# A retention-normalised attention feeding four sparse attention experts: gate logits folded into the state, new load runs, two-bank PSUM tiles and interleaved score row groups

## The chip, the cores and the metric

The kernel runs on one core of one Trainium2 chip. The metric is device time in microseconds of one launch; of the kernel before, three runs gave a median of 517.08 us (516.87 to 517.32).

## What is computed

Two blocks follow each other, in float32. B = 8 batches, H = 8 heads, S = 576 tokens, head dimension 64, E = 4 experts of head dimension 64, D = 512.

```python
# attention without softmax, per batch b and head h
kv  = einsum('bhsd,bhse->bhde', k, v)             # a 64x64 state per head
out = einsum('bhsd,bhde->bhse', q, kv)
x   = out / sqrt(mean(out*out, -1) + 1e-6) * g_norm      # -> x: B, S, H*64

# experts: the two largest of four gate logits per token
logits = x @ w_gate ; w = softmax over the top 2 logits
for e in range(4):
    qe, ke, ve = x @ wq[e], x @ wk[e], x @ wv[e]
    a  = softmax(causal(qe @ ke.T / 8))
    y += w_e * (a @ ve @ wo[e])                   # w_e = 0 where e is not chosen
```

All four experts are computed for all tokens, and the gate (zero where an expert is not chosen) scales their outputs.

## The kernel before

Every batch goes through two generators. `attention` (L157) is the first block, `moe_block` (L260) the second, and `moe_final` (L451) the output projection of a batch, put off until the next one. `run_interleaved` (L467) issues `moe_block` of batch b and calls one step of `attention` of batch b+1 for every four of its steps; before that loop `attention` of batch 0 runs alone (L489), and in the last round `moe_block` has no partner. Every engine takes its instructions in the order that results; the framework, which sets all semaphores, moves single instructions a little where its own plan finds them not ready.

`load_qkv` (L145) brings one batch's q, k and v by five token blocks (four of 128, one of 64): fifteen DMAs on SP's queue, all in runs of one token of one head, 256 bytes. Batch b+2 is loaded when batch b begins. The weights are loaded and scaled by g_norm before the first batch (L112 to L143).

`attention`: for each of four head pairs it transposes q (p_qT, L170), copies it to SBUF on ACT (L174), accumulates k-transposed times v over the tokens (p_kv, L177, 64 of 128 rows in the last block) and copies the two diagonal 64x64 blocks to kv2_all on DVE (L186, L187). Then, for each token block: out (p_out, L212, eight instructions of 128 columns, as a float32 product is two), squares on ACT (L220), sums on DVE (L222), mean plus epsilon (L229), the power -0.5 on POOL (rstd, L238), and the product x_tok on DVE (L245). Two blocks later `flush_one` (L196) transposes x_tok (p_xT), ACT copies it (L202), and DVE rounds it to xT_r (L203), the form in which the experts' matmuls read it.

`moe_block`: the gate logits are a float32 product of wg_f and xT (p_lt, L266), four rows high, transposed back to tokens (p_log, L276); L285 to L309 make the gates. Then follow ve of all experts (p_v, L322), `moe_final` of the batch before (p_y, L455; y_sb on DVE, L463; the store, L464), and for each of two expert pairs: projections (p_proj, L346, segments of 512 and 64 columns), copies to qTp and kTp (L358), scores transposed (p_sc, L371: first all of one expert, on rows 0 to 63, then all of the other, on rows 64 to 127, nine each), exponentials on ACT (L378), the causal mask on POOL (L384), then per query block and expert p_O (L409), a reciprocal (L417) and the scaling by reciprocal and gate (O_sc, L418), and a transpose (p_OT, L430) which ACT copies to OT_all (L446). Pair 1 starts its projections when pair 0 is through.

PSUM is one pool of eight one-bank buffers (L90).

## Time and profile before

| | us |
|---|---|
| median of three runs | 517.08 |
| span of the profiled execution | 515.2 |
| TensorE busy (matmul) | 400.2 |
| weight loads, beside them | 285.5 |
| DVE busy | 197.3 |
| ACT busy | 173.9 |
| POOL busy | 124.2 |

The profile is of one execution; no separate time of it is given beside its span of 515.2 us, and the median of the runs lies 1.9 us above that. Engines run side by side, so their times do not add up. PE is the matmul side of TensorE, PEld its weight loads. "Idle before <- X" is time in which the engine had nothing to do until X was finished. The input's 28.3 MB and the output's 9.4 MB pass over SP's queue.

### The profile page before, as it was taken

How to read it: one execution, taken by the hardware profiler on the slowest of the kernel's cores; microseconds unless marked ns; L12 is line 12 of the kernel's file. 1: busy time of each engine (PE TensorE's matmuls, PEld its weight loads, DVE VectorE, ACT ScalarE, POOL GpSimd, SP SyncE). 2: the span in 40 equal slices, each digit the busy share in tenths (PEclk: the TensorE clock that was granted, in tenths of full speed). 3: DMA queues.
4: the chain of work that ended last, by engine and by line, in shares of the span. 5: the costliest groups of instructions: out<-in, count | busy, mean ns of one | idle time of the engine just before them, and what ended most of it. 6: DMA issues, size and time to landing. Idle time of an engine off the chain costs nothing.

```text
span 515.2 us, 7111 instructions
## 1 busy us (share of the span) xinstructions
PE 400.2 (78%) x2472; PEld 285.5 (55%) x2472; DVE 197.3 (38%) x717; ACT 173.9 (34%) x569; POOL 124.2 (24%) x234
## 2 busy tenths in 40 slices
PE   0066696959969899679968799679968799679884
PEld 0055285726758467554757368454757367564661
DVE  1104334354252342543443442543433542543523
ACT  0013143611514215252246215251245215251440
POOL 3004202430132302351043302351043302340220
PEclk9999799869955599797988699796988699796866
DMA  8999908801390015900295014900200011000202
GB/s 168 206 195 204 206 13 160 118 1 42 108 205 15 2 41 128 199 2 0 92 182 96 1 41 119 207 3 0 87 7 1 1 42 52 0 2 1 93 0 92
DMA packets 125107, 40.31 MB, mean 78 GB/s; under 512 B 120208, under 2 KB 120208, under 8 KB 125072
## 3 DMA queue, kind: packets, MB, share of 16 engines
q1 hardware_dynamic: 125072, 39.87, 38.8%
q8 instruction: 19, 0.31, 0.3%
q14 instruction: 16, 0.13, 0.1%
HBM read 30.42 MB, written 9.44 MB: 77 GB/s over the span
## 4 chain that ended last, share of the span: by engine, by line
PE 56%; DVE 13%; POOL 11%; ACT 8%; issue 5%; DMA 3%; SPq 3%; POOLq 0%; DVEq 0%; ACTq 0%
POOL rstd L238 11%; PE p_kv L177 10%; PE p_lt L266 9%; PE p_proj L346 9%; PE p_out L212 5%; PE p_v L322 4%; PE p_qT L97 4%; DVE O_sc L418 4%; PE p_O L409 4%; PE p_y L455 3%; DVE x_tok L245 3%; PE p_sc L371 3%; ACT PT L378 3%; DVE sumsq L222 3%; ACT sq L220 2%
## 5 line engine op out<-in xcount | busy, mean ns | idle before, releaser
L384 POOL TENSOR_SCALAR_AFFINE_SELECT PT<-PT 128x128 bf16<-128x128 bf16 (+1 forms) x160 | 44.0, 290 | 195.4 <-ACT PT L378 191.0
L238 POOL TENSOR_TENSOR rstd<-msq,neg_half 128x8 f32<-128x8 f32 (+1 forms) x40 | 65.8, 1645 | 102.3 <-DVE msq L229 98.8
L378 ACT ACTIVATE PT<-p_sc 128x64 bf16<-128x64 f32 (+5 forms) x288 | 65.1, 341 | 14.5 <-PE p_sc L371 13.8
L409 PE MATMUL p_O<-vext,PT 128*128 128x65 bf16 (+2 forms) x480 | 43.5, 232 | 22.0 <-DVE x_tok L245 20.3
L371 PE MATMUL p_sc<-qTp,kTp 64*128 64x64 f32 (+5 forms) x288 | 49.3, 305 | 6.7 <-ACT kTp L358 4.2
L212 PE MATMUL p_out<-kv_all,qT_all 128*128 128x128 f32 (+1 forms) x320 | 52.8, 318 | 2.1 <-ACT PT L378 2.1
L245 DVE TENSOR_TENSOR x_tok<-p_out,rstd 128x512 f32<-128x512 f32 (+1 forms) x40 | 27.6, 689 | 65.3 <-POOL rstd L238 65.3
L177 PE MATMUL p_kv<-v_b,k_b 128*128 128x128 f32 (+1 forms) x320 | 51.7, 300 | 0.0
L97 PE MATMUL p_OT<-ident_b,O_sc 128*128 128x128 bf16 (+1 forms) x80 | 21.8, 273 | 38.4 <-DVE O_sc L418 38.1
L97 PE MATMUL p_qT<-ident_f,q_b 128*128 128x128 f32 (+1 forms) x160 | 28.6, 288 | 29.1 <-DMA q_b<-in_q_dram 29.1
L266 PE MATMUL p_lt<-xT,wg_f 128*4 128x64 f32 (+1 forms) x128 | 50.9, 564 | 0.0
L418 DVE TENSOR_SCALAR O_sc<-p_O,invr,gate 128x64 bf16<-128x64 f32 (+1 forms) x160 | 49.8, 334 | 1.6 <-PE p_OT L97 0.6
L409 PEld LDWEIGHTS <-PT 128*128 128x128 bf16 (+2 forms) x480 | 31.8, 124 | 30.8 <-POOL PT L384 11.1
L371 PEld LDWEIGHTS p_sc<-qTp,kTp 64*128 64x128 f32 (+1 forms) x288 | 39.3, 188 | 16.0 <-ACT kTp L358 5.8
L212 PEld LDWEIGHTS p_out<-kv_all,qT_all 128*128 128x128 f32 (+1 forms) x320 | 44.8, 209 | 5.8 <-ACT PT L378 3.5
L220 ACT ACTIVATE sq<-p_out 128x512 f32<-128x512 f32 (+1 forms) x40 | 23.8, 596 | 66.4 <-PE p_out L212 58.9
L222 DVE TENSOR_REDUCE sumsq<-sq 128x8 f32<-128x512 f32 (+1 forms) x40 | 27.2, 680 | 47.8 <-ACT sq L220 47.8
L177 PEld LDWEIGHTS p_kv<-v_b,k_b 128*128 128x128 f32 (+1 forms) x320 | 41.5, 194 | 6.3 <-issue 0.2
L174 ACT COPY qT_all<-p_qT 128x512 f32<-128x512 f32 x64 | 23.0, 419 | 61.5 <-PE p_qT L97 61.5
L186 DVE COPY kv_all<-p_kv 64x64 f32<-64x64 f32 x32 | 6.9, 216 | 90.1 <-PE p_kv L177 87.3
L97 PEld LDWEIGHTS p_qT<-ident_f,q_b 128*128 128x128 f32 (+1 forms) x160 | 19.4, 143 | 37.4 <-DMA q_b<-in_q_dram 19.9
L97 PE MATMUL p_xT<-ident_f,x_tok 128*128 128x128 f32 (+1 forms) x160 | 30.8, 330 | 8.7 <-DVE x_tok L245 5.8
(53 smaller groups left out, 419.9 us busy)
## 6 DMA issues: line engine op xcount, KB each, us to landing
q_b<-in_q_dram SPq DMA_DIRECT2D x32, 256.0 KB, 5.0
k_b<-in_k_dram SPq DMA_DIRECT2D x32, 256.0 KB, 5.0
v_b<-in_v_dram SPq DMA_DIRECT2D x32, 256.0 KB, 5.1
out_dram<-y_sb SPq DMA_DIRECT2D x32, 256.0 KB, 2.1
q_b<-in_q_dram SPq DMA_DIRECT2D x8, 128.0 KB, 5.1
k_b<-in_k_dram SPq DMA_DIRECT2D x8, 128.0 KB, 4.8
v_b<-in_v_dram SPq DMA_DIRECT2D x8, 128.0 KB, 4.4
out_dram<-y_sb SPq DMA_DIRECT2D x8, 128.0 KB, 2.3
```

The costliest lines, as they stand in the source:

```text
L97: nc.tensor.transpose(out_ap, in_ap, ident[:npart, :npart])
L177: nc.tensor.matmul(p_kv[:, :], lhsT=kb[:nt, i, 2 * hp : 2 * hp + 2, :].rearrange("p h d -> p (h d)"), rhs=vb[:nt, i, 2 * hp : 2 * hp + 2, ...
L212: nc.tensor.matmul(p_out[:nt, hp * P : (hp + 1) * P], lhsT=qT2_all[:, hp, t0 : t0 + nt], rhs=kv2_all[:, hp, :], start=True, stop=True,)
L238: nc.gpsimd.tensor_tensor(out=rstd[:nt, :], in0=msq[:nt, :], in1=neg_half[:nt, :], op=AluOpType.pow,)
L245: nc.vector.tensor_tensor(out=x_tok[:nt, :].rearrange("p (h d) -> p h d", h=H), in0=p_out[:nt, :].rearrange("p (h d) -> p h d", h=H), in1= ...
L266: nc.tensor.matmul(p_lt[:, :], lhsT=wg_f[:, c, :], rhs=xT_sb[:, c, slo:shi], start=(c == 0), stop=(c == NCH - 1),)
L346: nc.tensor.matmul(p_proj[:, :], lhsT=wsrc[:, c, 2 * pr : 2 * pr + 2, :].rearrange("p e f -> p (e f)"), rhs=xT_r[:, c, plo:phi], start=(c ...
L371: nc.tensor.matmul(p_sc[:nk, :], lhsT=kT_pair[pb : pb + Hd, t0 : t0 + nk], rhs=qT_pair[pb : pb + Hd, lo:hi], start=True, stop=True,)
L378: nc.scalar.activation(PT[:nk, off + (lo - t0) : off + (hi - t0)], p_sc[:nk, :], ACTF.Exp, scale=scale,)
L384: nc.gpsimd.affine_select(out=PT[:nk, off : off + nk], in_=PT[:nk, off : off + nk], compare_op=AluOpType.is_ge, fill=0.0, base=0, pattern= ...
L409: nc.tensor.matmul(p_O[:nq, :], lhsT=PT[:nkk, col : col + nq], rhs=v_ext[:nkk, kbi, e, :], start=(kbi == 0), stop=(kbi == qci),)
L418: nc.vector.tensor_scalar(out=O_sc[:nq, el, :], in0=p_O[:nq, 0:Hd], scalar1=invr[:nq], scalar2=gate[:nq, qci, e : e + 1], op0=AluOpType.mu ...
```

## The change

The whole body is rewritten into `stage1` (the first block), `stage2` (the second) and `final`; `weave` issues them by costs written into the yields. What changes:

- The loads come first, before the weights; k and v of 512 tokens in runs of four tokens (1 KB in DRAM, four pieces of 256 bytes in SBUF), one DMA for each head, the last 64 tokens into tiles of their own, padded with zeros; q as before. For batch 0, k and v come in steps of two heads. The order of tokens in k and v does not matter to the sum.
- The state gets four more columns per head: kv times w_gate, by transposing kv (p_kt) and one short product (p_kg). p_out is then 136 columns wide for each head pair, and its extra columns, scaled by rstd and summed over heads on DVE, are the gate logits. p_lt and p_log go.
- x is written as float32r by ACT alone; q's copies go to DVE, y's copies to ACT; epsilon is a 65th column of the squares; x's transpose follows one block behind.
- PSUM is split: three buffers of two banks (p_proj, p_sc, p_O, p_out) and two of one bank (all else).
- Projections in halves of 288 columns. Scores of both experts of a pair alternate row by row group, into two banks, with one exponential and one mask for both.
- Both pairs' projections and scores come first, then the output of the batch before, then p_O of pair 0 and pair 1; reciprocal, gate and scaling take several query blocks at once, and the five transposes of a pair go together.

Of the lines that go, most stand in the kernel printed above; of the new ones these matter here:

```diff
+        def main(dst, src, h0, h1):
+            for h in range(h0, h1):
+                nc.sync.dma_start(
+                    dst[:, :, h, :],
+                    src[b, h, 0 : NF * P, :].rearrange("(p j) d -> p j d", j=NF),
+                )
...
+        step = 2 if fine else H
+        for h0 in range(0, H, step):
+            main(kt, k, h0, h0 + step)
+            main(vt, v, h0, h0 + step)
+            if h0 == 0:
+                rem(kr[b % 2], k)
+                rem(vr[b % 2], v)
+        for i, (t0, nt) in enumerate(blocks):
+            nc.sync.dma_start(
+                qt[:nt, i, :, :], q[b, :, t0 : t0 + nt, :].rearrange("h p d -> p h d")
+            )
+        return qt, kt, vt
...
-    ps = ctx.enter_context(tc.tile_pool(name="ps", bufs=8, space=bass.MemoryType.PSUM))
...
+    ps2 = ctx.enter_context(tc.tile_pool(name="ps2", bufs=3, space=bass.MemoryType.PSUM))
+    ps1 = ctx.enter_context(tc.tile_pool(name="ps1", bufs=2, space=bass.MemoryType.PSUM))
+
+    def big(name):
+        return ps2.tile([P, 2, 512], FP32, tag="big", name=name)
+
+    def small(shape, name, dtype=FP32):
+        return ps1.tile(shape, dtype, tag="small", name=name)
...
+        p_kv = small([P, NCH, P], "p_kv")
+        for c in range(NCH):
+            kv_pair(p_kv, c, kb, vb, kr[b % 2], vr[b % 2])
+        kv_copy(p_kv, kvb, kv2)
+        yield 4.3
+        q_block(0)
+        yield 0.5
+        p_kt = small([P, NCH, P], "p_kt")
+        for c in range(NCH):
+            nc.tensor.transpose(p_kt[:, c, :], kv2[:, c, :], ident_f[:])
+        kt_sb = s1.tile([P, NCH, P], FP32, tag="kvT", name="kvT")
+        nc.vector.tensor_copy(out=kt_sb[:], in_=p_kt[:])
+        yield 0.5
+        q_block(1)
+        yield 0.5
+        p_kg = small([P, NCH, 2, E], "p_kg")
+        for c in range(NCH):
+            nc.tensor.matmul(
+                p_kg[:, c, :, :].rearrange("p a e -> p (a e)"),
+                lhsT=kt_sb[:, c, :],
+                rhs=wg_bd[:, c, :, :].rearrange("p a e -> p (a e)"),
+                start=True,
+                stop=True,
+            )
+        nc.vector.tensor_copy(out=kvb[:, :, :, Dh:GW], in_=p_kg[:])
...
+        def x_flush():
+            i, xt = pend.pop(0)
+            t0, nt = blocks[i]
+            p_x = small([P, NCH, P], "p_x")
+            for c in range(NCH):
+                nc.tensor.transpose(
+                    p_x[:, c, :nt], xt[:nt, c * P : (c + 1) * P], ident_f[:nt, :nt]
+                )
+            nc.scalar.copy(xT[:, :, t0 : t0 + nt], p_x[:, :, :nt])
...
+            po = p_o[:nt, :, 0 : 4 * GW].rearrange("p k (h g) -> p k h g", g=GW)
+            sq = sqs[i % 3]
+            nc.scalar.activation(
+                sq[:nt, :, 0:Dh].rearrange("p (k h) d -> p k h d", k=2),
+                po[:, :, :, 0:Dh],
+                ACTF.Square,
+                scale=1.0 / (Dh**0.5),
+            )
+            ms = blk.tile([P, H], FP32, tag="ms", name="ms")
+            nc.vector.tensor_reduce(ms[:nt], sq[:nt], axis=AX_X, op=AluOpType.add)
+            rstd = blk.tile([P, H], FP32, tag="rstd", name="rstd")
+            nc.gpsimd.tensor_tensor(
+                out=rstd[:nt], in0=ms[:nt], in1=neg_half[:nt], op=AluOpType.pow
+            )
+            xt = blk.tile([P, D], FP32, tag="x_tok", name="x_tok")
+            rb = rstd[:nt].rearrange("p (k h) -> p k h", k=2).unsqueeze(3)
+            nc.vector.tensor_tensor(
+                out=xt[:nt].rearrange("p (k h d) -> p k h d", k=2, h=4),
+                in0=po[:, :, :, 0:Dh],
+                in1=rb.to_broadcast([nt, 2, 4, Dh]),
+                op=AluOpType.mult,
+            )
+            gl = blk.tile([P, H, E], FP32, tag="gl", name="gl")
+            nc.vector.tensor_tensor(
+                out=gl[:nt].rearrange("p (k h) e -> p k h e", k=2),
+                in0=po[:, :, :, Dh:GW],
+                in1=rb.to_broadcast([nt, 2, 4, E]),
+                op=AluOpType.mult,
+            )
+            nc.vector.tensor_reduce(
+                lg8[:nt, i, 0:E],
+                gl[:nt].rearrange("p h e -> p e h"),
+                axis=AX_X,
+                op=AluOpType.add,
+            )
+            pend.append((i, xt))
+            yield 0.9
+            if len(pend) > 1:
+                x_flush()
+                yield 0.45
...
+                p_p = big("p_proj")
+                for c in range(NCH):
+                    for s in range(2):
                         nc.tensor.matmul(
+                            p_p[:, s, 0:HALF],
+                            lhsT=w_r[nm][:, c, 2 * pr : 2 * pr + 2, :].rearrange("p e f -> p (e f)"),
+                            rhs=xT[:, c, s * HALF : (s + 1) * HALF],
...
+            def piece(parts):
+                p_s = big("p_sc")
+                o = 0
+                for kb, lo, hi in parts:
+                    for el in range(2):
+                        pb = slice(el * Hd, (el + 1) * Hd)
                         nc.tensor.matmul(
+                            p_s[:, el, o : o + hi - lo],
+                            lhsT=kTp[pb, kb * P : (kb + 1) * P],
+                            rhs=qTp[pb, lo:hi],
                             start=True,
                             stop=True,
                         )
+                    o += hi - lo
+                kb, lo, hi = parts[0]
+                d0 = strip_off[kb] + lo - kb * P
+                nc.scalar.activation(PT[:, :, d0 : d0 + o], p_s[:, :, 0:o], ACTF.Exp, scale=scale)
...
+            piece([(0, 0, HALF)])
+            mask(0)
+            yield 0.25
+            piece([(0, HALF, S)])
+            yield 0.25
+            piece([(1, P, S)])
+            mask(1)
+            yield 0.35
+            piece([(2, 2 * P, S)])
+            mask(2)
+            yield 0.25
+            piece([(3, 3 * P, S), (4, 4 * P, S)])
+            mask(3)
+            mask(4)
+            yield 0.2
+            res["PT", pr] = PT
...
+            groups = ((0, (0, 1, 2)), (1, (3, 4)))
+            for bank, qcs in groups:
+                for n, qc in enumerate(qcs):
+                    s0, nq = blocks[qc]
+                    for el in range(2):
+                        for kb in range(qc + 1):
+                            nk = blocks[kb][1]
+                            col = strip_off[kb] + s0 - kb * P
+                            nc.tensor.matmul(
+                                p_O[:nq, bank, (2 * n + el) * (Hd + 1) : (2 * n + el + 1) * (Hd + 1)],
+                                lhsT=PT[:nk, el, col : col + nq],
+                                rhs=vx[:nk, kb, 2 * pr + el, :],
+                                start=(kb == 0),
+                                stop=(kb == qc),
+                            )
+                    yield 0.11 * (qc + 1)
+                for sub in ((qcs,) if bank == 0 else ((3,), (4,))):
+                    nq = blocks[sub[0]][1]
+                    n0, nn = sub[0] - qcs[0], len(sub)
+                    po = p_O[:nq, bank, n0 * 2 * (Hd + 1) : (n0 + nn) * 2 * (Hd + 1)].rearrange(
+                        "p (n f) -> p n f", f=Hd + 1
                     )
+                    iv = inv[:nq, sub[0] : sub[0] + nn, :]
+                    nc.vector.reciprocal(iv.rearrange("p n e -> p (n e)").unsqueeze(2), po[:, :, Hd : Hd + 1])
+                    nc.vector.tensor_tensor(
+                        out=iv, in0=iv, in1=gate[:nq, sub[0] : sub[0] + nn, 2 * pr : 2 * pr + 2],
+                        op=AluOpType.mult,
                     )
+                    nc.vector.tensor_tensor(
+                        out=osc[:nq, sub[0] : sub[0] + nn, :, :].rearrange("p n e f -> p (n e) f"),
+                        in0=po[:, :, 0:Hd],
+                        in1=iv.rearrange("p n e -> p (n e)").unsqueeze(2).to_broadcast([nq, 2 * nn, Hd]),
+                        op=AluOpType.mult,
                     )
+            res["osc", pr] = osc
...
+        yield from proj(0)
+        yield from scores(0)
+        yield from proj(1)
+        yield from scores(1)
+        if prev_y is not None:
+            yield from prev_y
+        yield from pv(0)
+        yield from o_t(0)
+        yield from pv(1)
+        yield from o_t(1)
...
+    W1, W2 = 16.0, 17.0
+
+    def weave(main, side):
+        a = s = 0.0
+        live = side is not None
+        for c in main:
+            a += c / W2
+            while live and s < a:
                 try:
+                    s += next(side) / W1
                 except StopIteration:
+                    live = False
```

## Rows read from the trace of the kernel before

**Rows 1.** The page's forty slices of the span: TensorE's busy tenths.

```profile
...
PE   0066696959969899679968799679968799679884
...
```

**Rows 2.** The table by stretch: busy us of each engine, granted clock, DMA share.

```profile
...
0.00:31.30 31.30, 2.24 (x6) 0.98 (x6) 3.09 (x5) 1.87 (x2) 4.47 (x16) 1.00 0.96 186
...
350.70:408.80 58.10, 48.44 (x311) 34.51 (x311) 24.11 (x89) 21.42 (x72) 14.89 (x27) 0.85 0.06 21
...
```

**Rows 3.** Waits over the span: who for whom, us in total, times, longest.

```profile
...
DVE x_tok L245 <- POOL rstd L238: 65.3, 40, 2.3
...
PE p_OT L97 <- DVE O_sc L418: 38.1, 40, 5.4
...
PE p_O L409 <- DVE x_tok L245: 20.3, 12, 2.1
...
```

**Rows 4.** The chain that ended last, in order of time: start, us, what.

```profile
...
18.18 1.29 SPq L151
...
31.30 2.00 PE p_kv L177 x8
...
41.33 1.11 PE p_out L212 x8
...
58.58 5.29 PE p_lt L266 x8
...
466.82 5.97 PE p_lt L266 x8
...
504.53 0.98 PE p_y L455 x2
506.25 2.08 DMA out_dram<-y_sb
...
```

**Rows 5.** Timeline of one batch on TensorE: start, us, line, tile, count.

```profile
...
350.67 6.49 PE L266 MATMUL p_lt<-xT,wg_f 128*4 128x512 f32 x16
...
359.56 0.80 PE L97 MATMUL p_qT<-ident_f,q_b 128*128 128x128 f32 x5
360.29 1.57 PE L177 MATMUL p_kv<-v_b,k_b 128*128 128x128 f32 x10
361.80 1.20 PE L322 MATMUL p_v<-wv_r,xT_r 128*128 128x256 f32 x8
...
365.95 1.58 PE L455 MATMUL p_y<-wo_pairs,OT_all 128*128 128x512 bf16 x6
367.46 1.56 PE L346 MATMUL p_proj<-xT_r,wq_r 128*128 128x512 f32 x8
...
376.82 1.16 PE L212 MATMUL p_out<-kv_all,qT_all 128*128 128x128 f32 x8
...
382.69 0.77 PE L409 MATMUL p_O<-vext,PT 128*128 128x65 bf16 x14
...
386.55 2.02 PE L212 MATMUL p_out<-kv_all,qT_all 128*128 128x128 f32 x8
...
```

**Rows 6.** Timeline of the last batch: scores and their exponentials.

```profile
...
482.19 3.58 PE L371 MATMUL p_sc<-qTp,kTp 64*128 64x512 f32 x18 [0.31 <-ACT kTp L358]
482.79 3.79 ACT L378 ACTIVATE PT<-p_sc 128x512 bf16<-128x512 f32 x18 [0.53 <-PE p_sc L371]
...
```

**Rows 7.** DVE by line and form: count, busy us, mean ns of one.

```profile
...
L418 DVE TENSOR_SCALAR O_sc<-p_O,invr,gate 128x64 bf16<-128x64 f32 x128 | 40.4, 336 | 1.3 <-PE p_OT L97 0.6
L245 DVE TENSOR_TENSOR x_tok<-p_out,rstd 128x512 f32<-128x512 f32 x32 | 22.1, 691 | 50.9 <-POOL rstd L238 50.9
...
L417 DVE RECIPROCAL invr<-p_O 128x1 f32<-128x1 f32 x128 | 18.0, 158 | 13.6 <-PE p_O L409 12.7
...
```

**Rows 8.** All engines by line and form: two exponentials and POOL's pow.

```profile
...
L238 POOL TENSOR_TENSOR rstd<-msq,neg_half 128x8 f32<-128x8 f32 x32 | 52.7, 1648 | 98.8 <-DVE msq L229 95.3 <-DVE invr L417 3.6
...
L378 ACT ACTIVATE PT<-p_sc 128x64 bf16<-128x64 f32 x128 | 31.9, 251 | 0.0
...
L378 ACT ACTIVATE PT<-p_sc 128x512 bf16<-128x512 f32 x32 | 19.2, 599 | 9.4 <-PE p_sc L371 9.4
...
```

More of the change, by code (lines that the diff above doesn't have):

```diff
@@ L56 @@
[L56 to L81 removed]
+    NF = S // P
@@ L83 @@
+    REM = S - NF * P
+    NB = NF + 1
+    HALF = S // 2
+    blocks = [(i * P, min(P, S - i * P)) for i in range(NB)]
+    scale = 1.0 / (Hd**0.5)
+    strip_w = [S - t0 for t0, _ in blocks]
+    strip_off = [sum(strip_w[:i]) for i in range(NB)]
+    strips = sum(strip_w)
+    GW = Dh + E
     const = ctx.enter_context(tc.tile_pool(name="const", bufs=1))
-    wts = ctx.enter_context(tc.tile_pool(name="wts", bufs=1))
+    wst = ctx.enter_context(tc.tile_pool(name="wst", bufs=2))
     qkvp = ctx.enter_context(tc.tile_pool(name="qkv", bufs=2))
-    attn = ctx.enter_context(tc.tile_pool(name="attn", bufs=2))
@@ new lines @@
+    loads = {0: load_qkv(0, fine=True)}
+    g_wide = const.tile([P, 1], FP32, name="g_wide")
+    for r in range(P // Dh):
+        nc.sync.dma_start(g_wide[r * Dh : (r + 1) * Dh, :], g_norm.unsqueeze(1))
+    wg_st = const.tile([P, NCH, E], FP32, name="wg_st")
+    nc.sync.dma_start(wg_st[:], moe_w_gate.rearrange("(c p) e -> p c e", p=P))
+    wg_bd = const.tile([P, NCH, 2, E], FP32, name="wg_bd")
+    nc.gpsimd.memset(wg_bd[:], 0.0)
+    for hh in range(2):
+        pp = slice(hh * Dh, (hh + 1) * Dh)
+        nc.vector.tensor_scalar_mul(
+            out=wg_bd[pp, :, hh, :], in0=wg_st[pp], scalar1=g_wide[pp]
+        )
@@ L260, in moe_block, with kv_pair @@
-    def moe_block(b, res, fin_state, deferred=None):
-        xT_sb, xT_r = res["xT"]
-        lgT = moe.tile([E, S], FP32, tag="lgT", name="lgT")
-        for (slo, shi) in segS:
-            p_lt = psum([E, shi - slo], name="p_lt")
+            wo_st[:, pr, :], moe_wo[2 * pr : 2 * pr + 2].rearrange("two d m -> (two d) m")
+        )
+    wo_b = const.tile([P, EP, D], BF16, name="wo_b")
+    nc.vector.tensor_copy(out=wo_b[:], in_=wo_st[:])
+    def kv_pair(p_kv, c, kb, vb, krem, vrem):
+        for j in range(NF + 1):
+            if j < NF:
+                lk, rv = kb[:, j, 2 * c : 2 * c + 2, :].rearrange("p h d -> p (h d)"), vb[:, j, 2 * c : 2 * c + 2, :]
+            else:
+                lk, rv = krem[:, 2 * c : 2 * c + 2, :].rearrange("p h d -> p (h d)"), vrem[:, 2 * c : 2 * c + 2, :]
+            nc.tensor.matmul(
+                p_kv[:, c, :], lhsT=lk, rhs=rv, start=(j == 0), stop=(j == NF)
+            )
@@ L265, in moe_block @@
             for c in range(NCH):
                 nc.tensor.matmul(
-                    p_lt[:, :],
-                    lhsT=wg_f[:, c, :],
-                    rhs=xT_sb[:, c, slo:shi],
-                    start=(c == 0),
-                    stop=(c == NCH - 1),
-                )
-            nc.scalar.copy(lgT[:, slo:shi], p_lt[:, :])
-        p_log = psum([P, NB, E], name="p_log")
-        for i, (t0, nt) in enumerate(blocks):
-            pe_transpose(p_log[:nt, i, :], lgT[:, t0 : t0 + nt], E)
@@ new lines, in o_t @@
+        def o_t(pr):
+            osc = res["osc", pr]
+            p_t = small([P, S], "p_OT", BF16)
+            for qc, (s0, nq) in enumerate(blocks):
+                nc.tensor.transpose(
+                    p_t[:, s0 : s0 + nq],
+                    osc[:nq, qc, :, :].rearrange("p e f -> p (e f)"),
+                    ident_b[:nq, :nq],
+                )
+            nc.scalar.copy(OT[:, pr, :], p_t[:])
+            yield 0.5
+        yield from proj(0)
+        yield from scores(0)
+        yield from proj(1)
@@ L459, in moe_final @@
[L459 to L475 removed]
+                    p_y[:nq, :], lhsT=OT[:, pr, s0 : s0 + nq], rhs=wo_b[:, pr, :],
@@ L476, in run_interleaved @@
+                    start=(pr == 0), stop=(pr == EP - 1),
+                )
+            y = ysb.tile([P, D], FP32, tag="y", name="y")
+            nc.scalar.copy(y[:nq, :], p_y[:nq, :])
+            nc.sync.dma_start(out[b, s0 : s0 + nq, :], y[:nq, :])
+            yield 0.45
+    W1, W2 = 16.0, 17.0
[5 more added lines that the diff above has]
+            while live and s < a:
                 try:
-                    next(gen_side)
+                    s += next(side) / W1
@@ L478, in run_interleaved @@
                 except StopIteration:
[L479 to L489 removed]
+                    live = False
+        if live:
+            for _ in side:
+                pass
+    res = {}
+    for _ in stage1(0, res):
         pass
[L491 removed]
+    y_gen = None
```

523 lines of the change are left out of this document (158 added, 365 removed).

## The prediction

> **What bounds the kernel now.** I read the page's slices first [rows 1]: TensorE is nearly idle for the first two of forty slices and then busy six to nine tenths throughout, in a pattern that repeats. The stage table [rows 2] gives the repeat: in one batch of 58.1 us TensorE is busy 48.44, DVE 24.11, ACT 21.42, POOL 14.89, at a mean granted clock of 0.85. So TensorE sets the pace, with 9.7 us idle. The waits [rows 3] say for what: over eight batches it waits 38.1 us for O_sc and 20.3 for x_tok, both DVE results, and DVE itself sits 65.3 us (40 times, 1.63 each) for POOL's pow. The chain in order of time [rows 4] cuts the span: the first batch's attention ends at 58.58, when p_lt begins; the seventh repeat ends at 466.8; the last batch, with nothing beside it, takes the 48.4 us left. Hence 515.2 = 58.6 + 7 x 58.3 + 48.4. The median, 517.08, is 1.9 above the span; I add 1.9 at the end as what lies around it.
>
> **TensorE's work in one batch, before and after.** Prices are instructions in a row at full clock [rows 5]: p_kv 1.57/10 = 0.157 us each, p_qT 0.80/5 = 0.16 (taken for p_xT and the new transposes too), p_v 1.20/8 = 0.15, p_proj 1.56/8 = 0.195, p_out 1.16/8 = 0.145, p_O 0.77/14 = 0.055 (p_OT likewise), p_y 1.58/6 = 0.263. The 18 score matmuls of a pair take 3.58 us [rows 6], 0.199 each, close to the 3.79 of their exponentials on ACT, so that price is ACT's pace as much as TensorE's.
>
> Kept: 40 p_qT and p_xT transposes 6.4, 40 p_kv 6.3, 20 p_v 3.0, 60 p_O 3.3, 10 p_OT 0.6, 10 p_y 2.6: 22.2 us. Besides these, before: 32 p_proj 6.2, 40 p_out 5.8, 36 scores 7.2, and the gate logits, 16 p_lt in 6.49 [rows 5] and about 0.6 more for p_log. Sum 48.5. The batch takes 58.3, so a gap of 9.8 us is left, as much as the table's idle time. (p_lt ran partly at half clock, since it follows the idlest stretch; whatever stands there next inherits that.)
>
> After:
> - Gate logits: p_lt and p_log go, 7.1. In their place four transposes of the state (0.64), eight short matmuls p_kg (no row has them; as p_kv, the nearest in kind, 1.3; between p_O and p_y, 0.055 and 0.263 each, so 0.4 to 2.1), and p_out of 136 columns instead of 128: 40 x 0.154 = 6.2.
> - p_proj: two halves of 288 columns instead of 512 and 64. A p_v of 256 columns is 0.15, p_proj's own mean 0.195; I take 0.16 (near p_v in width): 5.1. Bounds 4.8 to 6.2.
> - Scores: 24 matmuls instead of 36, 4.8 at the old pace. Bounds: 24 x 0.055 = 1.3 and the old 7.2.
>
> Sum 22.2 + 0.6 + 1.3 + 6.2 + 5.1 + 4.8 = 40.2, bounds 35.5 to 44.5.
>
> The row of the scores is for matmuls that stay in one half of the array's rows for a whole expert [rows 6]; the new order alternates the halves.
> The Trainium skill (TensorE: Matmul & The Clock Gate, "The mechanism") says that work in different row groups runs at once, each weight load beside the other's matmul. By it the 4.8 would be about 2.4, an estimate, and the time 387 - 7 x 2.4 = 370; no run so far shows it.
>
> **The other engines.** DVE: 20 O_sc at 0.336 and 20 reciprocals at 0.158 [rows 7], 9.9 us, become per pair 3 reciprocals, 3 products of as few columns (0.16) and products of 384, 128 and 128 columns (0.59, 0.39, 0.39, between 0.336 at 64 and 0.691 at 512): 4.7. Five y copies of 512 columns leave, as wide as x_tok (0.69), and five qT copies of that width come; the xT_r casts leave, and kvT and two short gate steps per block come. Net about -4 us of 24.1. ACT gains the y copies, loses the qT copies, and its exponentials go from 18 to 5 per pair: 0.251 us at 64 columns and 0.599 at 512 [rows 8] give 0.78 ns a column, 2.5 us for the pair's 3200, so the 18 in 3.79 cost 0.07 each beside it; five cost that at least and 0.2 at most: 2.9 to 3.5. POOL: the masks of two experts go together and the memsets of each batch leave; the five pows stay, 1.65 each [rows 8]. I cost all this at nothing: each of the three stays under 25 us, and TensorE's 40 hide it. Without that cover its price is what rivals 2 and 3 have.
>
> Queues: SP issues 23 loads a batch for 15, the slowest of before 1.29 us [rows 4], with the five stores behind them; 28 x 1.29 = 36 of 45 us, so nothing waits. A load two batches ahead enters a buffer that the previous repeat freed.
>
> **The gap.** Of the old 9.8, O_sc waits are 38.1/8 = 4.8 and x_tok waits 2.5. Output transposes now wait twice a batch, not ten times, but DVE still reduces, waits for pow and multiplies in one order: reduce 0.69, pow and its signals 1.85, product 0.69, two gate steps 0.32 = 3.55 per block (the reduction, of the same width, taken as the product). A transpose of x now follows one block behind, not two. Bound below: no wait left, 0. Above: the old 9.8 and 2 for half clock, at which eight p_out take 2.02 instead of 1.16 [rows 5]; it now falls on p_v and p_kv, which stand where p_lt stood, about 9 us of work. I take 5: 3 for waits (the DVE work behind p_O is halved) and that 2. Repeat 40.2 + 5 = 45 us.
>
> **Start.** The table shows 186 GB/s over the first 31.3 us [rows 2]. Old order: weights and all of q, k, v before p_kv at 31.30 [rows 4]. New: k and v of batch 0 (2.36 MB, 12.7 us), then q (1.18 MB, 6.3): q is in at about 20.5 with 1.5 for the first issue and landing. p_out before began at 41.33 and p_lt at 58.58: 17.2 for five blocks chained through pow; the new block trades a cast for the two gate steps, about even. With the last q transposes and their copy, 1.3: 20.5 + 1.3 + 17.2 = 39. Bounds: 35, if the 1 KB runs take a third off the 12.7 of k and v; 47, if DVE's weight casts, now behind these loads, stand in front of the first copies (1.6 MB, 8.5 us).
>
> **End.** 48.4 - 7.1 (p_lt and p_log, with the copies between them, to p_v) - 5 - 5 = 31. The first 5 is the last stores: the five blocks of y go through two buffers, each behind a store of 2.08 us [rows 4], 10.7 in all from 504.5; with four buffers it is 5 copies of 0.6, a store of 2.1 and 0.6 for signals. The second 5: projections of pair 1 beside the exponentials of pair 0, p_O of pair 0 beside those of pair 1. Bounds 27 to 40.
>
> **Sum.** 39 + 7 x 45 + 31 + 1.9 = 387 us.
>
> **Rivals.**
> 1. Waits nearly vanish: the period is TensorE's sum, 35.5 to 41, mid 38.5: 72 + 269 = 341 (320 to 359). For it: most of TensorE's 9.7 idle of 58 comes from two DVE waits, and alternating halves could shorten the scores. Against: pow stays in DVE's order. Chance 0.2.
> 2. DVE's chain becomes the bound of the second half of each batch. There five blocks (17.8) and both pairs' normalization (4.7) make 22.5 us, against 15.9 for the p_out, p_xT, p_y, p_O and p_OT in that stretch. With nothing hidden at its edges the period is 40.2 + 6.6 + 5 (half clock spreading) = 52: 436 (415 to 460). For it: the old DVE waits 1.63 us at every x_tok without other work between. Against: p_v and p_kv of the next repeat need little from DVE. Chance 0.18.
> 3. Slower: the one-bank pool falls from eight buffers to two, and p_q, p_kv, p_kt, p_kg, p_x, p_v, p_y, p_OT share it: 25 tiles a batch. A tile holds its buffer for fill, signal, copy and signal, bare 0.6 + 0.2 + 0.7 + 0.1 = 1.6 us: 25 x 1.6 / 2 = 20, hidden. If the copy queues behind others (a pow of 1.65, two exponentials) the price grows; it decides where 25 x r / 2 passes 63.6, the period that gives the old time: r = 5.1 us. Time 520 to 545. Against: a copy behind one pow and one product (3.3 us in all with the bare 1.6, less 0.7 of its own) stays under that. Chance 0.05.
> 4. Each change between half-height scores and full-height work pauses TensorE. The first p_sc of the last batch stands idle for 0.31 us, though that is put down to kTp [rows 6]; twenty changes a batch at that price are 6 us: 387 + 7 x 6 = 429. Against: before, scores stood among other work too, and full-height work begins behind them without an idle time. Chance 0.05.
> The Trainium skill ("TensorEngine Tiling (Array Packing)", "Key Properties") says that a change of tiling mode drains the array; no row here shows a drain by itself.
> 5. The longer load runs do nothing: the start stays at 39, as forecast; only the 35 falls away.
>
> **How the numbers follow.** Forecast 387 (366 to 408), chance 0.49; rivals 1 to 4 0.2, 0.18, 0.05 and 0.05, and 0.03 between 460 and the old time. Below 335 lies about a third of rival 1 (0.07), above 450 a fifth of rival 2, all of 3 and that 0.03 (0.12): range 335 to 450. Within 0.2% is what a measurement of this kernel can't tell from no change: 0.01. Faster 0.93; slower 0.06.
>
> **What would show it.** A repeat of 45 us with no p_lt; TensorE idle under 6 a batch; first p_out near 22 and first p_v near 39; after the last p_O no more than 7 us. Wrong, if DVE waits 8 us a batch for pow while TensorE waits for osc (rival 2), if p_q or p_y starts late behind its own copies (rival 3), or if the first DVE copies wait for weights.

## The result, and the profile after

The changed kernel takes 399.68 us (median of four runs, 397.35 to 401.06) against 516.98 (516.63 to 517.32) in the same session: ratio 0.774, 95% interval 0.770 to 0.778. The forecast was 387 (335 to 450): right in sign and within its range, but partly for wrong reasons. The profiled execution took 399.57, its span 397.9. Where single runs of a kernel lie more than 1.5% above its fastest, the medians below include them and the ratios do not.

The page's slices of the kernel after, busy tenths of TensorE and the clock it was granted [rows 1]:

```profile
...
PE   2686698786996689959997799959997799959984
...
PEclk9958589858999559995899669995899669985976
...
```

The repeat is about 4.5 slices long; in each, one or two fall to 5 or 6 tenths of the clock. The table by stretch [rows 2]: length, busy us of TensorE, weight loads, DVE, ACT, POOL, granted clock, DMA share, GB/s.

```profile
...
0.00:17.40 17.40, 8.70 (x42) 7.78 (x43) 0.40 (x3) 0.00 (x0) 7.77 (x26) 1.00 0.77 171
17.40:46.60 29.20, 18.78 (x95) 15.32 (x93) 15.60 (x41) 7.33 (x12) 8.16 (x5) 0.68 0.80 172
46.60:98.40 51.80, 41.94 (x293) 36.43 (x293) 21.07 (x71) 17.05 (x31) 11.88 (x15) 0.80 0.80 161
276.60:321.00 44.40, 38.50 (x289) 31.37 (x289) 19.13 (x64) 18.89 (x34) 11.85 (x15) 0.85 0.08 28
...
365.40:397.90 32.50, 24.71 (x164) 16.18 (x165) 6.60 (x27) 15.76 (x27) 3.73 (x10) 0.76 0.22 73
...
```

The first p_v starts at 46.6 (p_lt before: 58.6), seven repeats take 318.8 (before 408.2), the end 32.5 (48.4). So 117 us came off: 12 at the start, 89 in the repeats, 16 at the end. Waits over the span [rows 3]:

```profile
...
DVE x_tok L278 <- POOL rstd L273: 54.9, 39, 1.8
...
PE p_x L247 <- DVE gl L285: 28.1, 24, 2.4
...
PE p_out L255 <- DVE inv L452: 6.9, 3, 2.8
...
```

POOL's power by line and form [rows 8], with count, busy us, mean ns:

```profile
...
L273 POOL TENSOR_TENSOR rstd<-ms,neg_half 128x8 f32<-128x8 f32 x32 | 52.3, 1637 | 79.5 <-DVE ms L271 45.5 <-DVE inv L452 12.5 <-DVE lg L291 9.4
...
```

The first stretch of one repeat and its second half in steps of 5 us (columns as in the table above):

```profile
...
276.60:281.60 5.00, 5.00 (x27) 4.66 (x27) 0.99 (x5) 0.64 (x1) 0.00 (x0) 0.59 0.01 3
...
301.60:306.60 5.00, 3.04 (x30) 2.38 (x31) 3.04 (x11) 2.27 (x5) 1.88 (x3) 1.00 0.48 159
306.60:311.60 5.00, 3.16 (x44) 2.48 (x42) 2.44 (x8) 1.59 (x3) 3.06 (x2) 0.98 0.00 0
311.60:316.60 5.00, 3.92 (x20) 2.73 (x20) 2.44 (x14) 0.77 (x2) 0.21 (x1) 0.50 0.02 5
316.60:321.00 4.40, 3.74 (x27) 2.65 (x24) 2.58 (x14) 1.50 (x4) 1.63 (x1) 0.50 0.00 0
...
```

TensorE is busy 3 of 5 us for ten us, and then the clock is at the lower level, half, for the rest of the repeat and the first four us of the next. The chain in order of time [rows 4] says what sets those 20 us:

```profile
...
301.28 0.69 DVE x_tok L278
...
302.43 0.69 DVE ms L271
...
303.26 1.65 POOL rstd L273
...
304.93 0.69 DVE x_tok L278
...
306.26 0.57 DVE ms L271
...
306.97 1.65 POOL rstd L273
...
308.64 0.69 DVE x_tok L278
...
```

A block every 3.7 us: reduction, power, product, gate steps, and TensorE transposes when the product is there (the wait is put down to gl, DVE's next instruction).

### The profile page after: what moved, and what is told of

Its sections match the earlier page's. It is cut to its first block, busy times and chain, and to the rows that moved or that the text cites. A ratio compares the mean times of both kernels' runs of the same rounds, so it can differ in the third digit from the quotient of the medians.

```text
span 397.9 us, 6154 instructions
## 1 busy us (share of the span) xinstructions
PE 323.5 (81%) x2296; PEld 263.1 (66%) x2304; DVE 157.6 (40%) x513; ACT 152.9 (38%) x273; POOL 102.7 (26%) x146
## 2 busy tenths in 40 slices
DMA packets 126125, 40.25 MB, mean 101 GB/s; under 512 B 121233, under 2 KB 121233, under 8 KB 126097
## 4 chain that ended last, share of the span: by engine, by line
PE 50%; DVE 16%; POOL 14%; ACT 10%; issue 3%; SPq 3%; DMA 2%; ACTq 0%; POOLq 0%; DVEq 0%
POOL rstd L273 14%; PE p_kv L177 11%; PE p_proj L356 11%; PE p_v L338 7%; ACT PT L394 6%; DVE x_tok L278 6%; DVE ms L271 6%; PE p_out L255 5%; PE p_q L201 4%; PE p_x L247 3%; PE p_sc L384 3%; SPq L113 2%; ACT sq L264 2%; PE p_kg L225 2%; PE p_O L436 2%
## 5 line engine op out<-in xcount | busy, mean ns | idle before, releaser
L273 POOL TENSOR_TENSOR rstd<-ms,neg_half 128x8 f32<-128x8 f32 (+1 forms) x40 | 65.4, 1635 | 115.1 <-DVE ms L271 78.1
L399 POOL TENSOR_SCALAR_AFFINE_SELECT PT<-PT 128x256 bf16<-128x256 bf16 (+1 forms) x80 | 29.8, 383 | 164.4 <-ACT PT L394 163.6
L255 PE MATMUL p_out<-kvx,qT 128*128 128x136 f32 (+1 forms) x320 | 59.3, 332 | 8.2 <-DVE inv L452 6.9
L255 PEld LDWEIGHTS p_out<-kvx,qT 128*128 128x128 f32 (+1 forms) x320 | 48.6, 211 | 17.8 <-issue 10.9
L247 PE MATMUL p_x<-ident_f,x_tok 128*128 128x128 f32 (+1 forms) x160 | 32.4, 333 | 34.4 <-DVE gl L285 28.1
L394 ACT ACTIVATE PT<-p_sc 128x576 bf16<-128x576 f32 (+3 forms) x80 | 50.5, 713 | 8.9 <-PE p_sc L384 8.8
L177 PE MATMUL p_kv<-v_b,k_b 128*128 128x128 f32 x256 | 42.9, 323 | 8.4 <-DMA v_b<-in_v_dram 7.3
L278 DVE TENSOR_TENSOR x_tok<-p_out,rstd 128x512 f32<-128x512 f32 (+1 forms) x40 | 27.6, 690 | 54.9 <-POOL rstd L273 54.9
L177 PEld LDWEIGHTS p_kv<-v_b,k_b 128*128 128x128 f32 x256 | 40.2, 238 | 9.0 <-issue 9.0
L206 DVE COPY qT<-p_q 128x512 f32<-128x512 f32 (+1 forms) x40 | 25.4, 638 | 20.8 <-PE p_q L201 20.2
L338 PE MATMUL p_v<-wv_r,xT 128*128 128x256 f32 (+1 forms) x160 | 31.8, 335 | 0.5 <-ACT xT L250 0.5
L356 PE MATMUL p_proj<-xT,wq_r 128*128 128x288 f32 x128 | 31.5, 366 | 0.3 <-ACT PT L394 0.3
L384 PE MATMUL p_sc<-qTp,kT 64*128 64x288 f32 (+2 forms) x192 | 26.9, 344 | 2.7 <-ACT PT L394 1.7
```

What stands on the lines that cost most here:

```text
L177: nc.tensor.matmul(p_kv[:, c, :], lhsT=lk, rhs=rv, start=(j == 0), stop=(j == NF))
L247: nc.tensor.transpose(p_x[:, c, :nt], xt[:nt, c * P : (c + 1) * P], ident_f[:nt, :nt])
L255: nc.tensor.matmul(p_o[:nt, c // 2, (c % 2) * 2 * GW : (c % 2 + 1) * 2 * GW], lhsT=qT[:, c, t0 : t0 + nt], rhs=kvb[:, c, :, :].rearrange(" ...
L273: nc.gpsimd.tensor_tensor(out=rstd[:nt], in0=ms[:nt], in1=neg_half[:nt], op=AluOpType.pow)
L278: nc.vector.tensor_tensor(out=xt[:nt].rearrange("p (k h d) -> p k h d", k=2, h=4), in0=po[:, :, :, 0:Dh], in1=rb.to_broadcast([nt, 2, 4, Dh]),
L338: nc.tensor.matmul(p_v[:nt, :], lhsT=xT[:, c, t0 : t0 + nt], rhs=w_r["v"][:, c, :, :].rearrange("p e f -> p (e f)"), start=(c == 0), stop= ...
```

## Experiments

Theory: POOL's power inside DVE's order sets the second half of each repeat, and its half clock the first four us of the next. Rivals: the gate's folding is what counts; a pool of PSUM buffers limits; the start is lost to weight casts and loads. Times stand beside 399.68.

**The power left out: rstd is a DVE product in place of POOL's power.**

```diff
-            nc.gpsimd.tensor_tensor(
-                out=rstd[:nt], in0=ms[:nt], in1=neg_half[:nt], op=AluOpType.pow
+            nc.vector.tensor_tensor(
+                out=rstd[:nt], in0=ms[:nt], in1=neg_half[:nt], op=AluOpType.mult
```

> Leaves out the power -0.5: a product on DVE stands in POOL's place, so the numbers that follow are other ones, with the same shapes. Theory A (the idle time left in a batch is DVE waiting for POOL's pow between a block's sum and its product): the 54.9 us of x_tok waits and most of TensorE's 28.1 us of waits for gl go, the repeat falls from 44.5 to about 40, the start by 5 to 7, in all 358 to 368 us. Rival B (TensorE's own work at the clock it gets sets the repeat, and the waits lie beside it): repeat 43.5 or more, in all 388 to 395 through the start alone.

329.97 us (ratio to before 0.637, 0.632 to 0.643; its output is another, since the power is missing). The repeat by the table of stretches:

```profile
...
223.70:260.90 37.20, 35.08 (x288) 29.25 (x289) 19.84 (x69) 18.73 (x35) 3.74 (x10) 0.95 0.25 60
...
```

37.2 instead of 44.4, at 0.95 of the clock. The theory holds, with about twice the expected size.

**The old gate logits** (p_lt and p_log back; p_kt, p_kg and the gate steps out):

```diff
-    GW = Dh + E
+    GW = Dh
...
+            p_lt = small([E, shi - slo], "p_lt")
...
...
+                nc.tensor.matmul(
+                    p_lt[:, :], lhsT=wg_f[:, c, :], rhs=xTf[:, c, slo:shi],
...
```

> Undoes one part: the gate logits come from p_lt and p_log at the head of stage2 as before, p_kt, p_kg, the four extra columns and the gate steps go, xT is kept in float32 too and rounded by DVE; three y buffers instead of four make room. Theory A (folding takes real TensorE time off the repeat, worked out as 7.1 less 2.5): 7 x 4.6 + 3 for start and end, 430 to 440 us. Rival B (p_lt would lie in idle time at the border of two batches, and the gate steps gone from DVE's chain give back): 400 to 412.

407.95 us (403.23 to 408.16; 0.784, 0.778 to 0.791), in theory B's range: folding is worth 8 us by the medians, 6 between the fastest runs. The start on TensorE's timeline:

```profile
...
20.83 1.13 PE L237 MATMUL p_out<-kvx,qT 128*128 128x128 f32 x8 [0.51 <-DVE kvx L181]
...
39.82 5.66 PE L286 MATMUL p_lt<-xTf,wg_f 128*4 128x512 f32 x16
...
46.24 0.74 PE L323 MATMUL p_v<-wv_r,xT 128*128 128x256 f32 x4
```

Its repeat in the table by stretch:

```profile
...
271.00:317.40 46.40, 40.44 (x301) 30.11 (x302) 18.95 (x56) 20.78 (x39) 11.76 (x15) 0.90 0.08 26
...
```

This repeat is 46.4 (45.5 to 46.9 for those behind the first; 44.4 with folding). TensorE's busy time falls by only 1.9 with folding (40.44 to 38.50), as its clock falls too (0.90 to 0.85). At the start p_out comes 6.5 us earlier than with folding and p_lt takes that back: no gain there.

**PSUM split the other way** (two two-bank buffers, four of one bank):

```diff
-    ps2 = ctx.enter_context(tc.tile_pool(name="ps2", bufs=3, space=bass.MemoryType.PSUM))
-    ps1 = ctx.enter_context(tc.tile_pool(name="ps1", bufs=2, space=bass.MemoryType.PSUM))
+    ps2 = ctx.enter_context(tc.tile_pool(name="ps2", bufs=2, space=bass.MemoryType.PSUM))
+    ps1 = ctx.enter_context(tc.tile_pool(name="ps1", bufs=4, space=bass.MemoryType.PSUM))
```

> PSUM split the other way: two buffers of two banks and four of one bank, instead of three and two. Theory A (neither pool is what TensorE waits for; no row names a copy out of the small pool among its long waits): 396 to 404. Rival B (two one-bank buffers hold TensorE back, as the third rival of the prediction had it): faster by 10 or more, under 390. Rival C (the two-bank pool is the tight one, a block holds its tile through pow): slower, over 410.

436.68 us (0.842, 0.835 to 0.849), 37 us slower. TensorE's waits:

```profile
...
PE p_x L247 <- DVE x_tok L278: 24.3, 18, 3.0
PE p_out L255 <- DVE inv L452: 16.0, 6, 3.1
PE p_out L255 <- ACT PT L394: 9.1, 6, 1.5
...
```

In the kernel after, the first two are 5.0 and 6.9. The large pool is the tight one: p_out holds a buffer from its matmul to the product behind the power. The edit changes both pools at once, so it does not show by itself that the small one has room.

**The product emitted one block later** (x_half pops block i-1 behind the power of block i):

```diff
...
+            half.append((i, nt, po, rstd))
+            if len(half) > 1:
+                x_half()
```

> Same work, other order: the product x_tok and the gate steps of a block are issued one block later, after the sum of the next block, and its transpose follows in the same step. Theory A (DVE's wait for pow is the cause): the sum of the next block fills the wait, the repeat falls by 2 to 4 us, in all 372 to 388. Rival B (the waits lie beside TensorE's work, and a tile of p_out held one block longer costs as much): 396 to 412.

397.28 us (396.22 to 401.99; 0.768, 0.761 to 0.774), no difference to be told, and short of theory A's 372 to 388. DVE's wait stays:

```profile
...
DVE x_tok L258 <- POOL rstd L300: 54.4, 40, 1.8
...
```

In DVE's timeline the product stands right behind the power again, ahead of the next block's sum: the framework's planner moved it back, so this says nothing of a later product.

**The power on ACT**, exp(-0.5 ln ms), with one table set for both functions:

```diff
+    nc.scalar.preload_act_table_set("natural_log_exp_and_others")
...
-            nc.gpsimd.tensor_tensor(
-                out=rstd[:nt], in0=ms[:nt], in1=neg_half[:nt], op=AluOpType.pow
-            )
+            nc.scalar.activation(rstd[:nt], ms[:nt], ACTF.Ln)
+            nc.scalar.activation(rstd[:nt], rstd[:nt], ACTF.Exp, scale=-0.5)
```

> The power -0.5 is made on ACT, as exp(-0.5 ln ms), in two instructions of 128x8, with one table set loaded at the start that has both functions; POOL has only the masks left. Theory A (what costs the 70 us that the run without the power showed is the length of the detour reduction - pow 1.65 us - product, in DVE's order): two short ACT instructions, of which the shortest exponential of 0.251 us is the nearest row, and one more signal make 0.7 of the 1.65, so rather more than half of the 70 us comes back: 340 to 360 us, a repeat of 38.5 to 41. Theory B (the detour is late because its engine is shared): on ACT the two instructions queue behind exponentials of 0.6 us and copies, two of them in a row, so DVE waits as long as before: 385 to 405 us, and DVE's waits for rstd stay near 1.4 us each.

336.23 us (330.23 to 337.39, against 517.61 before): theory A, a little better than its 340 to 360, and far from B. By line on ACT (count, busy us, mean ns of one):

```profile
...
L275 ACT ACTIVATE rstd<-rstd 128x8 f32<-128x8 f32 x32 | 6.9, 216 | 0.8
L274 ACT ACTIVATE rstd<-ms 128x8 f32<-128x8 f32 x32 | 6.9, 215 | 6.5 <-DVE ms L272 6.5
```

DVE's wait for it, over the span:

```profile
...
DVE x_tok L278 <- ACT rstd L275: 9.1, 16, 1.0
...
```

Two instructions of 0.215 replace one of 1.637, and the wait falls from 54.9 to 9.1. It is nearly as fast as no power at all.

**Short load runs** in the new order:

```diff
-                    src[b, h, 0 : NF * P, :].rearrange("(p j) d -> p j d", j=NF),
+                    src[b, h, 0 : NF * P, :].rearrange("(j p) d -> p j d", p=P),
```

> As the changed kernel, but k and v are read in runs of one token (256 bytes, tokens 128 apart in a partition) instead of four (1 KB); the number of DMAs, their size and the order stay. Rival 5 of the prediction (the longer runs do nothing, since the packets are still 256 bytes, 121 thousand of them below 512 bytes): 396 to 404 us, p_kv of batch 0 through at 17 to 18 us. The other theory (runs of 1 KB read faster): p_kv of batch 0 through 3 to 4 us later, 403 to 408 us in all.

396.63 us (396.44 to 399.15; ratio 0.765, 0.760 to 0.770), p_kv of batch 0 through at 16.0, a little ahead of the 17.4 with runs of 1 KB: the 1-KB runs do nothing. The packets below 512 bytes number 121,233 in the kernel after and 121,232 here.

**Weights scaled on ACT, gate weights loaded first:**

```diff
...
-        nc.vector.tensor_scalar_mul(
-            out=wr[:].rearrange("p c e f -> p (c e f)"),
...
+        nc.scalar.mul(
+            wr[:].rearrange("p c e f -> p (c e f)"),
...
```

> As the changed kernel, but the three scaled weights are written by ACT instead of DVE and the gate's weights and g_norm are loaded ahead of q, k and v. Theory A (the first p_v came at 46.6 instead of the forecast 39 since DVE's weight casts stood among the block chains and p_kg waited for the gate's weights): first p_v at 39 to 42, the second as much earlier, 392 to 396 us. Theory B (the loads of batch 1 start behind the weights, whose staging buffers come free only with the casts, so the second p_v stays near 98): first p_v at 39 to 42, first period 55 to 58, 397 to 401 us.

398.79 us (396.82 to 399.47; 0.767, 0.762 to 0.772). The time is in theory B's range, but the first p_v came at 45.7, so neither theory's 39 to 42: the casts weren't what delayed the start, nor the gate's weights alone.

**Three staging buffers for the weights** (`wst`, bufs=3):

> As the changed kernel, with three staging buffers for the weights instead of two, so that SP's queue no longer stops at the third weight for the cast of the first. Theory A (the first period is 51.7 us instead of 44.5 since the loads of batch 1 start at 30.7): they start near 27 and the second p_v comes 3 to 5 us earlier, 394 to 398 us. Theory B (the first period is long for its TensorE and DVE work, casts included, and the loads only keep pace): under 1 us, 398 to 401 us.

397.84 us (392.42 to 400.37; 0.760, 0.751 to 0.769), the second group of p_v at 97.7 instead of 98.0, though SP's 4.2 us of waiting were gone: by that mark theory B. The median is in theory A's range by 0.2 us; the runs spread too far to tell it from the changed kernel's.

**Power on ACT with both start edits** (staging 3; g_norm and gate weights first, on ACT's queue):

```diff
...
-        nc.sync.dma_start(g_wide[r * Dh : (r + 1) * Dh, :], g_norm.unsqueeze(1))
...
+        nc.scalar.dma_start(g_wide[r * Dh : (r + 1) * Dh, :], g_norm.unsqueeze(1))
...
```

> The run with the power on ACT (336.2 us), with a third staging buffer for the weights and with g_norm and the gate's weights loaded first, over ACT's queue. Theory A (with the power short, the start is what is left to gain: p_kg of batch 0 waited 2.7 us for the gate's weights, and the loads of batch 1 stood 4 us behind the third weight): first p_v at 38 to 40 instead of 41.4, 328 to 334 us. Theory B (what comes earlier waits for the loads of the next batches, which keep DMA at 0.9 of its time until 85 us): 334 to 338 us.

332.45 us (331.55 to 337.84; ratio 0.644, 0.640 to 0.648), the lowest median of a kernel that computes the same, though its runs overlap those of the power on ACT alone. Start, first repeat and a later one by the table:

```profile
...
0.00:34.80 34.80, 21.20 (x133) 18.11 (x133) 15.04 (x40) 8.62 (x23) 7.77 (x26) 1.00 0.93 186
34.80:79.00 44.20, 36.74 (x280) 31.38 (x281) 20.60 (x68) 18.18 (x40) 3.75 (x10) 0.88 1.07 202
226.46:263.28 36.82, 34.75 (x289) 29.19 (x289) 19.45 (x63) 20.14 (x44) 3.75 (x10) 0.95 0.21 52
...
```

p_v starts 6.5 us earlier than with the power on ACT alone (41.4), and the first repeat gives most of it back (78.9 against 80.9). The time is in theory A's range, what became of the earlier start is theory B's; that the loads took it back is not shown, for DMA is at its full share in that repeat but no wait of TensorE's names a load.

**Power on ACT with the old gate logits:**

> The run with the power on ACT, with the gate logits made as before the change (p_lt and p_log put back, p_kt, p_kg and the two gate steps on DVE taken out, p_out 128 columns wide). Theory A (folding was worth little only because the detour through the power, not TensorE, set the repeat; now that TensorE is busy 34.7 of 36.8 us, its net 5 us a batch - p_lt and p_log about 6.5, less p_kt, p_kg and the wider p_out - show whole): 336 + 7 x 5 = 371, 360 to 380 us. Theory B (the logits cost TensorE little beside other work, and the longer chain of the state costs as much): 336 to 346 us, as the two kernels with the power on POOL lay 8 us apart.

360.47 us (357.35 to 363.32; 0.697, 0.692 to 0.702): at the lower edge of theory A's range, far from B's. A repeat:

```profile
...
209.00:249.20 40.20, 38.14 (x304) 28.49 (x304) 19.52 (x56) 21.08 (x49) 3.75 (x10) 1.00 0.49 119
...
```

Folding is now worth 24 us by the medians instead of 8 (27 between the fastest runs instead of 6): 3.4 in the repeats shown instead of 2.0, and all of it TensorE's busy time (38.14 to 34.75).

**Power on ACT, scores at full height** (keys in two zero-padded tiles):

```diff
-                            lhsT=kTp[pb, kb * P : (kb + 1) * P],
-                            rhs=qTp[pb, lo:hi],
+                            lhsT=kTp[el][:, kb * P : (kb + 1) * P],
+                            rhs=qTp[:, lo:hi],
```

> The run with the power on ACT, but the two experts' keys lie in two tiles padded with zeros in the other's 64 rows, so that each score matmul takes all 128 rows and none stands beside another; keys are copied in two instructions of half height, two pairs of such tiles. Theory A (matmuls in different row groups run at once, as 2048 columns in 0.74 us suggest): 3200 columns a pair at the projections' rate (8 x 288 columns in 1.16 us) take 1.6 us instead of half that, 16 pairs: 13 us more, 345 to 352 us, and the first piece of 2048 columns takes over 0.9 us. Theory B (nothing runs at once, or the exponentials set the pace of the scores anyway): 334 to 340 us.

345.16 us (344.69 to 345.77; 0.669, 0.666 to 0.673), 9 us above the median with the power on ACT alone: theory A, at the edge of its range. A repeat, to be set against the 36.82 above:

```profile
...
235.98:274.05 38.07, 36.04 (x289) 30.69 (x289) 19.45 (x63) 21.38 (x46) 3.75 (x10) 0.95 0.19 48
...
```

TensorE is busy 1.29 us longer with the same number of instructions (1.6 expected), and the repeat 1.25 longer. The score matmuls of one repeat alone, at half height (power on ACT, start edits) and at full height:

```profile
...
226.46:263.28 36.82, 3.40 (x24) 1.89 (x24) 6.29 (x10) 0.95 0.21 52
...
236.00:274.00 38.00, 5.42 (x24) 3.45 (x24) 6.28 (x10) 0.95 0.19 48
...
```

A single one lasts as long in both (median 0.362 and 0.346 us), but at half height 24 of them cover 3.40 us instead of 5.42, and in the trace's single records the two of a pair start 3 to 5 ns apart: row groups do run at once.

**The kernel before with the power on ACT**, the same two lines in its `attention`:

> The kernel before the change, with the power -0.5 made on ACT in two instructions as in the runs above, and nothing else altered. Theory A (the old kernel hid the detour through the power: x's transpose followed two blocks behind and eight PSUM buffers let p_out run ahead, so of DVE's 65.3 us of waits TensorE saw 20.3): 495 to 512 us, and the change with the power on ACT is worth more than with it on POOL. Theory B (the detour cost the old kernel as much as the new one, some 64 us, half clock included): 445 to 465 us, and the change is worth about 117 us with either.

459.30 us (456.62 to 461.08; ratio 0.886, 0.878 to 0.893): theory B. TensorE's waits over the span:

```profile
...
PE p_OT L97 <- DVE O_sc L415: 28.3, 30, 1.9
...
PE p_O L406 <- DVE x_tok L242: 1.0, 6, 0.2
```

A repeat in its table by stretch:

```profile
...
202.90:254.10 51.20, 45.66 (x309) 32.41 (x309) 23.95 (x89) 22.92 (x81) 7.32 (x24) 0.93 0.45 93
...
```

The old kernel paid 58 us for the same power, its repeat 51.2 instead of 58.1. So the change is worth 117 us with the power on POOL and 123 with it on ACT: the two gains add up.

## Why the prediction was right, and where it was not

**The repeat, forecast 45, measured 44.4 to 44.6**: two errors of opposite sign.

- *TensorE's sum, 40.2, was too large by over 5.* With the power on ACT the same work takes 34.75 us busy (the same 289 instructions), part of it still at half clock. I divided a row's duration by its count and added. By that measure I was nearly right: in that repeat (power on ACT, start edits) the busy times of the twelve tiles, each taken alone, add up to 40.8. But the rows of neighbours overlap at their edges, by 6.0 us in all. On TensorE's timeline eight p_out last 1.09 us, and the next row starts 0.93 behind their start:

```profile
...
248.76 1.09 PE L256 MATMUL p_out<-kvx,qT 128*128 128x136 f32 x8
249.69 1.03 PE L492 MATMUL p_y<-wo_b,OT 128*128 128x512 bf16 x4
...
```

  Single terms missed both ways: the scores, priced at ACT's pace, 4.8, are 3.40, p_proj 6.16 instead of 5.1, p_OT 1.53 instead of 0.6. That the same adding met the busy time before (48.5 against 48.44) was luck: it counted the overlaps, and its full-clock prices left out that the clock was 0.85 there. With the power on ACT the old kernel's TensorE is busy 45.66 in a repeat.
- *p_kv got cheaper by the change itself, which I had not forecast*: 6.3 before and 6.3 forecast, 4.63 after. Its busy time in a repeat before, and in one at full clock with the power on ACT:

```profile
...
350.70:408.80 58.10, 6.30 (x40) 0.85 0.06 21
...
230.70:265.93 35.23, 4.63 (x40) 1.00 0.21 53
...
```

  The count is the same. In the trace's single records eight p_kv of 128 rows follow each other 0.112 us apart, but before the change the two of the last block, 64 rows high, started 0.205 and 0.214 behind the one ahead, and the first pair of each group, which stood behind a 64-row p_qT, 0.213 apart. After it the last block is padded to 128 rows, the four groups stand together, and at full clock all start 0.112 apart. So a change of height costs TensorE time that no idle time shows; no run takes the padding out alone.
- *The gap, 5, is 9.6 when the busy time with the power on ACT is taken for TensorE's work* (44.4 - 34.8). The detour through the power is 7.6 of it: 3.8 as idle time (5.9 of 44.4, against 2.1 of 36.8) and 3.75 as busy time at half clock. I had 3 and 2 for all of it.

**The block chain of 3.55 us was right** (3.65 and 3.71 between products), and DVE's net of about -4 us came out at -5 (24.1 to 19.1). What failed is that TensorE's work hides the chain. From the first p_x of a repeat to the next p_v are 18.7 us (302.12 to 320.86), and 12.3 in the kernel with the power on ACT (251.01 to 263.28): rival 2's mechanism, at about half of its price (6.5 of 11.8 us a repeat). Rival 1's time, 341, is what the kernel gives once the power leaves the chain (336 and 332): I named pow as what spoke against it, and that was the condition.

**Gate folding**, forecast at 4.8 us of TensorE a repeat net, is worth 2.0 with the power on POOL and 3.4 with it on ACT, in the repeats shown.

**Start, forecast 39, measured 46.6.** The mis-sized term is the way from the loads to the first p_out, which I priced as TensorE work alone. TensorE's timeline of the kernel after, with ACT's first instruction:

```profile
...
20.57 0.63 PE L217 MATMUL p_kt<-ident_f,kv 128*128 128x128 f32 x4 [2.74 <-ACT kv L187]
...
23.12 1.84 PE L225 MATMUL p_kg<-wg_bd,kvT 128*128 128x8 f32 x8 [1.28 <-DVE wg_bd L147]
...
27.32 5.08 PE L255 MATMUL p_out<-kvx,qT 128*128 128x136 f32 x24
...
46.57 1.22 PE L338 MATMUL p_v<-wv_r,xT 128*128 128x256 f32 x4
...
17.90 1.28 ACT L187 ACT_TABLE_LOAD   x1 [17.90 <-DVE kvx L184]
...
```

p_out starts at 27.3 instead of 21.8, and at 20.8 without the state's new chain (copy, transpose, copy, product, copy). But the chain by itself need not cost that. With the power on ACT and the start edits the whole chain stands there too, and p_out comes when I forecast it:

```profile
...
21.84 1.15 PE L256 MATMUL p_out<-kvx,qT 128*128 128x136 f32 x8
...
```

What held it up is two things that the chain waits for. ACT's table load, which before the change ran at 0.8 us, now stands in front of the first copy of kv; and p_kg waits for the gate's weights, which are loaded behind q, k and v. To take one away is not enough: with the table loaded at the start (power on ACT alone) p_out starts at 26.9, with the gate's weights loaded first at 26.6. The clock goes with it: 0.68 from 17.4 us to the first p_v in the kernel after, 1.00 over the whole start with the power on ACT and the start edits. The table load was moved only together with the power, so its share is read from these starts and not tried alone. The five blocks behind p_out took 19.3 instead of 17.2; with the power on ACT 14.5, with the start edits as well 13.0. Weight casts (my bound of 47) were not the cause: with them on ACT p_v came at 45.7.

**The first repeat, 51.8** by the table's bounds, was forecast like the others. The bound 98.4 lies 2.6 us behind the second batch's first p_v (95.79); from first p_v to first p_v the repeats are 49.2, 46.4, 45.2 and then 44.4 to 44.6. Neither the casts, the staging buffers nor the load runs move the first; with the power on ACT alone it is 39.6 against 36.8 later on, with the start edits as well 44.0. What makes it longer than its successors stays open.

**End, 31 against 32.5:** but 11 us pass after the last p_O (386.8 to 397.9), not 7.

By the table's bounds: start +7.6, first repeat +6.8, six repeats -3.0, end +1.5: 12.9, of the 12.7 between 387 and 399.7. That the repeats together came so near, 318.8 for 315, is luck: two errors of over 4 us a repeat took each other away.

**The other rivals.** 3 (the small pool): its time did not come, and over the whole span p_x waits 0.7 us for the copy that frees its tile; the run with four one-bank buffers was slower, but lost a two-bank one by the same edit. 4: no idle time stands ahead of the scores where they follow full-height work. TensorE's timeline of the last batch [rows 6]:

```profile
...
371.82 1.04 PE L492 MATMUL p_y<-wo_b,OT 128*128 128x512 bf16 x3
372.79 0.74 PE L384 MATMUL p_sc<-qTp,kT 64*128 64x288 f32 x6
373.46 0.60 PE L492 MATMUL p_y<-wo_b,OT 128*128 128x512 bf16 x2
...
```

Two p_y start 0.215 us apart, p_sc 0.310 behind the last one: 0.1 us at most for this change, not 0.3. 5 was right. The rule of the Trainium skill ("TensorE: Matmul & The Clock Gate", "The mechanism") that work in different row groups runs at once holds: the 2048 columns here take 0.74 us, and full height costs 1.25 us a repeat. My 2.4 by that rule was an estimate from the overpriced 4.8; the scores take 3.40.

How the gain of each repeat (13.9 us) divides was tried only for folding (2.0) and the score rows (1.25, with the power on ACT). What the new order, the grouped normalization, the padding and the pools are worth against the kernel before is not shown.

## What to carry to other kernels

A small instruction on a slow engine, in the middle of another engine's order, is to be priced by the chain it sits in, not by the waits of the bounding engine: there it appears again as idle time, and once more as half clock. What one edit is worth depends on the bound: folding gained some 8 us behind the power and 24 without it. When a new schedule is summed from the trace, use start-to-start distances of consecutive rows, not durations, and do not take a sum that meets the old busy time as proof of its prices: look at the clock under which that time was measured.
